# Two linear-attention and gMLP layers on one core: ScalarE issues the stores of the turned rows and of the gelu rows

## The chip, the core and the metric

The kernel runs on one core of one Trainium2 chip. The metric is the device time of one execution in microseconds. The core has a matrix engine (TensorE, PE in the profile), three engines for element-wise work (VectorE, DVE; ScalarE, ACT; GpSimd, POOL), and a sync engine (SyncE, SP) that computes nothing and here issues most of the DMAs. Every engine runs its own list of instructions in order. What ties the lists together are semaphores: an instruction waits until the semaphores of what it needs have reached given values. A DMA is issued by the instruction list of one engine (an instruction of its own, which first waits for what it has to read), runs beside the engines, and raises a semaphore when it has landed.

## The reference

Two pairs of layers, each with a layer norm ahead and a residual around it, on `x` of 2048 tokens by 512 features, all in fp32. First linear attention with 32 heads of 16 features:

```python
pq, pk = phi(q), phi(k)                       # phi(t) = (t + 1 if t > 0 else exp(t)) + 1e-6
kv  = einsum("bhsd,bhse->bhde", pk, v);  z = sum of pk over s
num = einsum("bhqd,bhde->bhqe", pq, kv); den = einsum("bhqd,bhd->bhq", pq, z) + 1e-6
x = x + (num / den) @ wo
```

Then a gMLP block with 2 x 896 inner features:

```python
z = gelu(layernorm(x) @ w_in);  z1 = z[..., :896];  z2 = layernorm(z[..., 896:])
g = einsum("ts,bsf->btf", w_sp, z2) + b_sp[None, :, None]
x = x + (z1 * g) @ w_out
```

Both blocks run twice with the same weights.

## The kernel before

**Precision.** Every fp32 product is made of three matmuls: both operands are split into a high and a low half, and `mm3` (L150 to L152) adds high·high, high·low and low·high. A high half is a copy on ACT (`high`, L136), a low half a subtraction on DVE (`low`, L139). So nearly every operand of PE passes through ACT and then DVE.

**Stages of a layer.** P1 goes over the 16 token tiles of 128 rows for K, Q and the sums of the attention. P2 goes over them again (`P2.run`, the token steps, step `s` from 1 to 18): it finishes attention, and makes the two halves of the gMLP's expansion. P4 multiplies by `w_sp` and then `w_out`. In the profile the token steps of layer 0 lie at about 155 to 330 us, those of layer 1 at about 838 to 1012 us.

**A token step** works on several token tiles at different stages. In program order, for a step `s` in the middle:

- `b(s)`: take the turned rows of attention's numerator for tile `s`, split them (ACT L136, DVE L139 on pages `pg`); `c(s-1)`: multiply the tile before by the folded weights (12 matmuls, 128x512); `c2`: DVE adds the result to the residual (L849); `c_stats`: the norm's statistics (DVE L265, L267, POOL L269 to L274).
- `a2(s+2)`: divide by the denominator (DVE L806 to L817) and store the rows for turning (`qt`, on SP).
- `c3(s-1)`: store the new residual (L857, on SP), normalise on ACT into a tile `z_turn` (L280), and store that for turning (`yt`, L316).
- `d(s-2)`: take the turned rows of an earlier `yt`, split them into `qd` (ACT L136, DVE L139); `e(s-3)`: multiply `qd` by the second half of the expansion's weights (24 matmuls, the form 128x448); `e2` to `e4`: gelu (ACT L906), sum of squares (L915), norm of an earlier tile (L280 on `z_z`).
- `f`, up to twice: one feature tile of the first half of the expansion, computed transposed for four token tiles at once (12 matmuls), gelu on ACT (L941), and a store to DRAM (L944), which P4 loads later. The target is a tile `z_out` for the first one in a step and a page `pg` for the second.
- `make.step` (layer 0 alone): sums of weight pieces, split on ACT and DVE and stored by SP (L231); loads for the steps to come.

**Turning.** A tile must be transposed between the two products. `Turn` does this for most tiles by way of DRAM: `store` (L316) writes the 128x512 rows as four blocks, `load` reads them back in another order, and DVE transposes blocks of 32x32 (L331). There are three kinds: `xt` in P1, `qt` and `yt` in P2. For `yt` (`xturn`) the tiles 0 to 3 of each layer are turned by PE instead, so 12 tiles per layer are stored and loaded.

**Order.** The program is written out by hand in this order; nothing reorders it. Each engine takes its instructions from the common text. Pages (`pg`, 23 of them) and other buffers are reused, and an instruction that writes one waits for the last reader, also when that is a DMA. Each DMA raises one of eight semaphores ("lanes", DMAHW0 to DMAHW7 for those of SP and ACT), and it waits for the DMA that used its lane before.

In the tail of the steps and in P4's start, `gelu_out` (L949 to L953) makes the same kind of gelu row; there the store is already issued by ACT (L952).

Of the kernel before, what the change touches and what calls it, by code (L numbers as in the profile page):

```python
# [91 lines left out]
def mixer_kernel(ctx: ExitStack, tc: tile.TileContext, x_in, wqkv, wo_d, win1_d, win2_d, wsp_d, bsp_d, wout_d,  # L92
                 ident_d, mask_d, out_d):
    nc = tc.nc
# [15 lines left out]
    def ztag(i, shape, kind, dtype=F32):  # L110
        t = main.tile(shape, dtype, tag=f"z{i}", bufs=1, name=f"z{i}_{kind}")
        ztile[i] = t
        return t
# [14 lines left out]
    z1s = {}  # L128
# [19 lines left out]
    def mm3(out, a, b, start, stop):  # L148
        (ah, al), (bh, bl) = a, b
        nc.tensor.matmul(out, ah, bh, start=start, stop=False)  # L150
        nc.tensor.matmul(out, ah, bl, start=False, stop=False)  # L151
        nc.tensor.matmul(out, al, bh, start=False, stop=stop)  # L152

    class Weight:


        def __init__(self, slots, shape, pieces, turned=False):
            self.slots, self.shape, self.pieces, self.turned = slots, shape, pieces, turned
            self.h = self.l = None
            self.raw = deque()  # L160
            self.n_load = self.n_split = 0
# [42 lines left out]
    class Make:  # L204
# [22 lines left out]
        def store(self, g):  # L227
            m = 2 * len(self.raw[g])
            h, l, p = self.part.pop(g)
            for n, t in enumerate((h, l)):  # L230
                nc.sync.dma_start(kept[:, m:m + 2, g, n, :], t.rearrange("p (m f) -> p m f", m=2))  # L231
            pages.put(p, l, lag=STORE)
# [21 lines left out]
    def w_in1():  # L254
        return Weight(bigs, [P, NF, 4, P], [win1_d[f] for f in range(NF)])
# [29 lines left out]
    def feats(ap, turned):  # L285

        return ap.rearrange("p (g c j) -> p c g j" if turned else "p (c g j) -> p c g j", g=4, c=4)
# [7 lines left out]
    class Turn:  # L295

        def __init__(self, name, by_pe, always=False):
            self.name, self.by_pe, self.always = name, by_pe, always  # L300
            self.held, self.d, self.raw = {}, {}, {}

        def turned(self, i):
# [3 lines left out]
        def store(self, i, src):  # L307
            if i in self.by_pe:
                if self.always:
                    s = pages.get(PAGE)  # L310
                    nc.scalar.activation(feats(s, False), feats(src, True), AF.Copy)
                    src = s
                self.held[i] = src
                return
            d = self.d[i] = dram.tile([512, P], F32, name=f"{self.name}_{i}")
            nc.sync.dma_start(d.rearrange("(g n) f -> n g f", g=4), src.rearrange("p (g f) -> p g f", g=4))  # L316

        def load(self, i):
            if i in self.d:
                self.raw[i] = load(self.d.pop(i).rearrange("(p m) f -> p (m f)", m=4))  # L320
# [452 lines left out]
    class P2:  # L773
        def __init__(self, p1):
            self.L = L = p1.L
            self.p1 = p1
            self.win1, self.win2 = w_in1(), p1.win2
            self.qturn, self.xturn = Turn(f"qt{L}", range(3), True), Turn(f"yt{L}", range(4))
            self.qp, self.qT, self.x, self.ms, self.xB, self.z, self.zms = {}, {}, {}, {}, {}, {}, {}
            self.fq = deque()  # L780
            self.fnext = []
            self.held = deque()
            self.S, self.T, self.Tp, self.X, self.zmean = {}, {}, {}, {}, {}
# [145 lines left out]
        def f(self, tag=None):  # L929
            if not self.fq:  # L930
                return False
            n, f = self.fq.popleft()
            h, l = self.xT[n]
            w = self.win1
            b = banks.get(PAGE)
            for c in range(4):
                mm3(b, (w.h[:, f, c, :], w.l[:, f, c, :]), (h[:, c, :], l[:, c, :]), c == 0, c == 3)
            if f == NF - 1 and n < 2:
                quads.put(*self.xT.pop(n))
            t = pages.get(PAGE) if tag is None or tag >= NT else ztag(tag, PAGE, "out")  # L940
            nc.scalar.activation(t, b, AF.Gelu_apprx_tanh)  # L941
            banks.put(b)
            z1s[self.L, n, f] = dram.tile(PAGE, F32, name=f"z1_{self.L}_{n}_{f}")
            nc.sync.dma_start(z1s[self.L, n, f], t)  # L944
            if id(t) in pages.held:
                pages.put(t, lag=STORE)
            return True
# [983 lines left out]
```

## Time and profile before

| | |
|---|---|
| median of 3 runs | 1363.74 us (1363.53 to 1364.71) |
| profiled execution | 1365.79 us, of which the span of the profile is 1364.1 us |
| PE busy | 1355.8 us (99%) |
| DVE, ACT, POOL busy | 991.1 us (73%), 676.3 us (50%), 484.0 us (35%) |
| granted TensorE clock, mean | 0.998 |
| DMA | 310.18 MB, mean 227 GB/s |
| `yt` stores | 24 of 256 KB, issued by SP, 2.6 us to landing (median) |
| gelu stores of L944 | 32 of 256 KB, issued by SP, 2.0 and 2.1 us to landing (medians) |
| gelu stores of L952 | 24 of 256 KB, issued by ACT, 3.2 us to landing (median) |

How to read the rows. A row of the timeline has the start in us from the span's start, the duration in us, engine, line, instruction, output and inputs by name, shapes, and in brackets the engine's idle time just before, with what ended it. `SPq` and `ACTq` are the instruction lists themselves, which issue DMAs. A row of the waits reads: who waited, for whom, us in total, times, longest. A row of the chain has start, duration and what; for a DMA the duration runs from its issue to its landing. A row of the windows has the stretch, its length, the busy time of PE, PE's weight loads, DVE, ACT and POOL with the number of instructions, the granted clock of TensorE, the busy share of the DMA engines and GB/s.

### The profile page before, as it was taken

How to read it: one execution, taken by the hardware profiler on the slowest of the kernel's cores; microseconds unless marked ns; L12 is line 12 of the kernel's file. 1: busy time of each engine (PE TensorE's matmuls, PEld its weight loads, DVE VectorE, ACT ScalarE, POOL GpSimd, SP SyncE). 2: the span in 40 equal slices, each digit the busy share in tenths (PEclk: the TensorE clock that was granted, in tenths of full speed). 3: DMA queues.
4: the chain of work that ended last, by engine and by line, in shares of the span. 5: the costliest groups of instructions: out<-in, count | busy, mean ns of one | idle time of the engine just before them, and what ended most of it. 6: DMA issues, size and time to landing. Idle time of an engine off the chain costs nothing.

```text
span 1364.1 us, 18420 instructions
## 1 busy us (share of the span) xinstructions
PE 1355.8 (99%) x6087; PEld 1133.3 (83%) x6087; DVE 991.1 (73%) x1518; ACT 676.3 (50%) x1149; POOL 484.0 (35%) x594
## 2 busy tenths in 40 slices
PE   9999999999999999999999999999999999999998
PEld 7888888878888888888888888888888888888887
DVE  7985777666866797976678757776757798978642
ACT  6875555456543343442456655555665534533310
POOL 2333376543276247426421133533220011412240
PEclk9999999999999999999999999999999999999999
DMA  5862478876698888795776534666577698569552
GB/s 186 243 204 88 124 258 290 275 254 188 210 345 297 285 287 281 269 370 185 229 255 196 192 96 124 190 225 226 202 215 269 195 324 323 195 198 314 218 183 87
DMA packets 181744, 310.18 MB, mean 227 GB/s; under 512 B 15696, under 2 KB 67920, under 8 KB 177552
## 3 DMA queue, kind: packets, MB, share of 16 engines
q1 hardware_dynamic: 166544, 251.45, 56.2%
q0 software_dynamic: 11504, 51.12, 10.4%
q10 hardware_dynamic: 3600, 6.42, 1.3%
q8 instruction: 48, 0.79, 0.2%
q14 instruction: 48, 0.39, 0.1%
HBM read 211.68 MB, written 97.26 MB: 226 GB/s over the span
## 4 chain that ended last, share of the span: by engine, by line
PE 88%; DVE 4%; ACT 3%; DMA 2%; issue 1%; POOL 1%; DVEq 0%; ACTq 0%; POOLq 0%; SPq 0%
PE bank L152 15%; PE bank L150 15%; PE bank L151 15%; PE bank L1631 9%; PE bank L1632 9%; PE bank L1633 9%; PE bank L1562 4%; PE bank L1564 4%; PE bank L1565 4%; PE bank L1008 1%; PE bank L1009 1%; PE bank L1007 1%; DVE pg L331 1%; DMA pg<-yt 1%; DMA yt<-z_turn 1%
## 5 line engine op out<-in xcount | busy, mean ns | idle before, releaser
L1631 PE MATMUL bank<-qd,pg 128*128 128x512 f32 x544 | 211.6, 389 | 0.0
L1632 PE MATMUL bank<-qd,pg 128*128 128x512 f32 x544 | 211.6, 389 | 0.0
L1633 PE MATMUL bank<-qd,pg 128*128 128x512 f32 x544 | 211.6, 389 | 0.0
L1478 DVE TENSOR_TENSOR qd<-qd,qd 128x1024 fp32r<-128x1024 f32 x104 | 141.7, 1363 | 64.4 <-ACT qd L1469 64.1
L1469 ACT ACTIVATE qd<-qd 128x1024 fp32r<-128x1024 f32 x104 | 110.1, 1059 | 133.3 <-DVE qd L1478 41.0
L152 PE MATMUL bank<-qd,pg 128*128 128x512 f32 x380 | 148.8, 391 | 0.1
L136 ACT ACTIVATE pg<-pg 128x512 fp32r<-128x512 f32 (+1 forms) x146 | 89.7, 620 | 109.8 <-DVE pg L331 36.8
L139 DVE TENSOR_TENSOR pg<-pg,pg 128x512 fp32r<-128x512 f32 (+1 forms) x143 | 107.7, 753 | 29.7 <-ACT pg L136 24.8
L1653 POOL TENSOR_TENSOR bg<-bg,pg 128x512 f32<-128x512 f32 x56 | 89.4, 1607 | 108.6 <-DMA pg<-z 100.0
L1633 PEld LDWEIGHTS bank<-qd,pg 128*128 128x128 f32 x544 | 102.1, 188 | 21.3
L1631 PEld LDWEIGHTS bank<-qd,pg 128*128 128x128 f32 x544 | 102.1, 188 | 21.1
L1632 PEld LDWEIGHTS bank<-qd,pg 128*128 128x128 f32 x544 | 102.1, 188 | 21.1
L1221 POOL TENSOR_TENSOR pg<-pg,pg 128x512 f32<-128x512 f32 x50 | 77.3, 1545 | 107.9 <-DMA pg<-in_wsp_dram 92.1
L150 PE MATMUL bank<-qd,pg 128*128 128x512 f32 x284 | 110.8, 390 | 0.0
L151 PE MATMUL bank<-qd,pg 128*128 128x512 f32 x284 | 110.6, 389 | 0.0
L150 PE MATMUL bank<-bg,qd 128*128 128x448 f32 x256 | 94.9, 371 | 1.9 <-ACT qd L136 1.9
L331 DVE STREAM_TRANSPOSE pg<-pg 128x512 f32<-128x512 f32 x79 | 86.3, 1093 | 13.6 <-DMA pg<-yt 11.6
L152 PE MATMUL bank<-bg,qd 128*128 128x448 f32 x256 | 94.5, 369 | 0.4 <-DVE qd L139 0.2
L151 PE MATMUL bank<-bg,qd 128*128 128x448 f32 x256 | 94.2, 368 | 0.0
L269 POOL TENSOR_SCALAR rs<-mv 128x1 f32<-128x1 f32 x63 | 31.7, 504 | 168.3 <-DVE mv L267 165.0
L150 PE MATMUL bank<-wo,qd 128*128 128x512 f32 x224 | 87.1, 389 | 0.0
L1562 PE MATMUL bank<-qd,pg 128*128 128x512 f32 x224 | 87.1, 389 | 0.0
(227 smaller groups left out, 3234.5 us busy)
## 6 DMA issues: line engine op xcount, KB each, us to landing
qd<-s SPq DMA_DIRECT2D x64, 512.0 KB, 4.1
qd<-n POOLq DMA_DIRECT2D x32, 1024.0 KB, 8.0
pg<-in_wsp_dram SPq DMA_DIRECT2D x92, 256.0 KB, 4.9
qd<-in_wsp_dram SPq DMA_DIRECT2D x40, 512.0 KB, 4.6
pg<-z SPq DMA_DIRECT2D x56, 256.0 KB, 4.1
n<-pg SPq DMA_DIRECT2D x55, 256.0 KB, 4.3
x<-pg SPq DMA_DIRECT2D x48, 256.0 KB, 2.7
pg<-x SPq DMA_DIRECT2D x48, 256.0 KB, 3.5
```

What stands on the lines that cost most here:

```text
L136: nc.scalar.activation(h, src, AF.Copy)
L139: nc.vector.tensor_sub(l, src, h.bitcast(F32))
L150: nc.tensor.matmul(out, ah, bh, start=start, stop=False)
L151: nc.tensor.matmul(out, ah, bl, start=False, stop=False)
L152: nc.tensor.matmul(out, al, bh, start=False, stop=stop)
L331: nc.vector.transpose(y.rearrange("p c (t m) -> p m c t", m=4), r.rearrange("p (m c j) -> p m c j", m=4, c=4))
L1469: nc.scalar.activation(wh, r, AF.Copy)
L1478: nc.vector.tensor_sub(wl, r, wh.bitcast(F32))
L1562: m(out[i], h[:, o, f], w[:, o, 0], start=first and name in ("P1", "P2", "P5"), stop=False, skip_group_check=True)
L1631: m(out, h[:, o], w[:, 0, j, :], start=start, stop=False, skip_group_check=True)
L1632: m(out, h[:, o], w[:, 1, j, :], start=False, stop=False, skip_group_check=True)
L1633: m(out, l[:, o], w[:, 0, j, :], start=False, stop=stop, skip_group_check=True)
```

## The change

`Turn` gets an argument for the engine that issues its stores; P2 passes ScalarE for `yt`, while `xt` and `qt` stay on SP. The store of `f` is issued by ScalarE too. The loads stay on SP.

```diff
-        def __init__(self, name, by_pe, always=False):
-            self.name, self.by_pe, self.always = name, by_pe, always
+        def __init__(self, name, by_pe, always=False, issue=nc.sync):
+            self.name, self.by_pe, self.always, self.issue = name, by_pe, always, issue
...
-            nc.sync.dma_start(d.rearrange("(g n) f -> n g f", g=4), src.rearrange("p (g f) -> p g f", g=4))
+            self.issue.dma_start(d.rearrange("(g n) f -> n g f", g=4), src.rearrange("p (g f) -> p g f", g=4))
...
-            self.qturn, self.xturn = Turn(f"qt{L}", range(3), True), Turn(f"yt{L}", range(4))
+            self.qturn, self.xturn = Turn(f"qt{L}", range(3), True), Turn(f"yt{L}", range(4), issue=nc.scalar)
...
-            nc.sync.dma_start(z1s[self.L, n, f], t)
+            nc.scalar.dma_start(z1s[self.L, n, f], t)
```

PE, DVE and POOL keep their instructions and their order. ACT's list grows by 56 stores, SP's shrinks by the same 56. Below is ACT's list in layer 0's step 12 (the step that begins at 268.97 us), before, from the normalisation into `z_turn` to the split of the next tile; in square brackets the semaphores that an instruction waits for:

```order
L280 ACTIVATE z10_turn_3025<-pg18_302_2686,nb_3016,rs_3013 128x4x4x32 [waits Pool_49]
L280 ACTIVATE z8_z0_2917<-z8_z0_2917,znb_2942,zrs_2941 128x896 [waits Activation_49]
L906 ACTIVATE z9_z0_3062,acc_3063<-bank6_99_3036 128x448 [waits DMAHW2_49,PE_49]
L906 ACTIVATE z9_z0_3062,acc_3063<-bank7_100_3049 128x448 [waits PE_49]
L941 ACTIVATE z14_out_3081<-bank4_101_3068 128x512 [waits PE_49]
L915 ACTIVATE pg16_335_3088,ss_3085<-z9_z0_3062,nm_3066 128x896 [waits DMAHW6_49,DVE_49]
L941 ACTIVATE pg12_336_3106<-bank0_102_3093 128x512 [waits DMAHW7_49,PE_49]
L136 ACTIVATE pg8_337_3112<-pg1_299_2680 128x512 [waits DMAHW3_49]
L136 ACTIVATE pg16_344_3132<-pg13_343_3130 128x512 [waits DVE_49,Activation_49]
```

The same place in the changed kernel:

```order
L280 ACTIVATE z10_turn_3025<-pg18_302_2686,nb_3016,rs_3013 128x4x4x32 [waits Pool_49]
L316 DMA yt0_11_3027<-z10_turn_3025 128x4x128 [waits DMAHW3_49,Activation_49]
L280 ACTIVATE z8_z0_2917<-z8_z0_2917,znb_2942,zrs_2941 128x896
L906 ACTIVATE z9_z0_3062,acc_3063<-bank6_99_3036 128x448 [waits PE_49]
L906 ACTIVATE z9_z0_3062,acc_3063<-bank7_100_3049 128x448 [waits PE_49]
L941 ACTIVATE z14_out_3081<-bank4_101_3068 128x512 [waits PE_49]
L944 DMA z1_0_1_4_3083<-z14_out_3081 128x512 [waits DMAHW7_49,Activation_49]
L915 ACTIVATE pg16_335_3088,ss_3085<-z9_z0_3062,nm_3066 128x896 [waits DMAHW4_49,DVE_49]
L941 ACTIVATE pg12_336_3106<-bank0_102_3093 128x512 [waits PE_49]
L944 DMA z1_0_1_5_3108<-pg12_336_3106 128x512 [waits DMAHW3_49,Activation_49]
L136 ACTIVATE pg8_337_3112<-pg1_299_2680 128x512
L136 ACTIVATE pg16_344_3132<-pg13_343_3130 128x512 [waits DVE_49,Activation_49]
```

Three stores now stand between the activations, each with two waits: for the activation just ahead of it, and for the DMA that used its lane before. The lane of the second z store (DMAHW3) is that of the `yt` store four activations earlier.

SP's list at the same place before, from the store of the `qt` rows to the load of the turned `yt` rows:

```order
L316 DMA qt0_14_3019<-pg21_321_2883 128x4x128 [waits DMAHW0_49,DVE_49]
L857 DMA x1_11_87<-pg18_302_2686 128x512 [waits DMAHW1_49]
L316 DMA yt0_11_3027<-z10_turn_3025 128x4x128 [waits DMAHW2_49,Activation_49]
L944 DMA z1_0_1_4_3083<-z14_out_3081 128x512 [waits DMAHW3_49,Activation_49]
L944 DMA z1_0_1_5_3108<-pg12_336_3106 128x512 [waits DMAHW4_49,Activation_49]
L231 DMA win1_sums_124<-pg7_324_2967 128x2x256 [waits DMAHW5_49]
L231 DMA win1_sums_124<-pg19_300_2682 128x2x256 [waits DMAHW6_49]
L132 DMA pg15_338_3115<-yt0_11_3027 128x512 [waits DMAHW7_49,DMAHW2_49,PE_49]
```

And in the changed kernel:

```order
L316 DMA qt0_14_3019<-pg21_321_2883 128x4x128 [waits DMAHW0_49,DVE_49]
L857 DMA x1_11_87<-pg18_302_2686 128x512 [waits DMAHW1_49]
L231 DMA win1_sums_124<-pg7_324_2967 128x2x256 [waits DMAHW2_49,Activation_49]
L231 DMA win1_sums_124<-pg19_300_2682 128x2x256 [waits DMAHW4_49]
L132 DMA pg15_338_3115<-yt0_11_3027 128x512 [waits DMAHW5_49,DMAHW3_49,PE_49]
```

The three stores are gone from SP's list, and the load of the turned rows (L132) follows two stores of `make` directly. The loads that come after it keep their order.

## Prediction

> **What bounds the kernel.** I read the page first, then who waits for whom on TensorE, then ACT and DVE in order of time in the token steps, and last SP.
>
> ```profile
> PE 1355.8 (99%) x6087; PEld 1133.3 (83%) x6087; DVE 991.1 (73%) x1518; ACT 676.3 (50%) x1149; POOL 484.0 (35%) x594
> PE   9999999999999999999999999999999999999998
> ```
>
> TensorE (PE) is busy for 1355.8 of 1364.1 us. So there is next to nothing to win, and every microsecond for which PE is made to wait is lost. What it waits for today:
>
> ```profile
> PE bank L150 <- ACT qd L136: 1.9, 2, 1.6
> PE bank L152 <- DVE qd L139: 0.2, 1, 0.2
> ```
>
> Both are operands of the matmul `e`, and they come out of the token steps. These two rows hold the only waits that this change can touch. Whether the new work on ACT is free depends on how much earlier than needed those operands are ready. DVE's L139 writes the low half of `qd`; L152 on a 128x448 form is the first matmul that reads it.
>
> ```profile
> 216.49 0.99 DVE L139 TENSOR_TENSOR qd<-pg,qd 128x512 fp32r<-128x512 f32 x1 [0.70 <-ACT qd L136]
> 230.63 1.21 DVE L139 TENSOR_TENSOR qd<-pg,qd 128x512 fp32r<-128x512 f32 x1 [0.70 <-ACT qd L136]
> 221.35 0.36 PE L152 MATMUL bank<-bg,qd 128*128 128x448 f32 x1
> 231.89 0.47 PE L152 MATMUL bank<-bg,qd 128*128 128x448 f32 x1
> 258.48 0.47 PE L152 MATMUL bank<-bg,qd 128*128 128x448 f32 x1 [0.23 <-DVE qd L139]
> 282.07 0.47 PE L150 MATMUL bank<-bg,qd 128*128 128x448 f32 x1 [0.37 <-ACT qd L136]
> 293.18 0.47 PE L150 MATMUL bank<-bg,qd 128*128 128x448 f32 x1 [1.57 <-ACT qd L136]
> ```
>
> In layer 0 the operand of the matmul at 221.35 was ready at 216.49 + 0.99 = 217.48, a lead of 3.87 us. For the next one it was ready at 231.84 and read at 231.89: the lead is gone. From there on PE runs on the heels of ACT and DVE, with 0.23, 0.37 and at last 1.57 us of waiting. So in the second half of layer 0's steps, whatever delays ACT and DVE delays PE.
>
> What ACT and DVE do in one such step (ACT first, then DVE):
>
> ```profile
> 268.97 0.63 ACT L136 ACTIVATE qd<-pg 128x512 fp32r<-128x512 f32 x1 [4.10 <-DVE pg L331]
> 269.51 0.80 ACT L280 ACTIVATE z_turn<-pg,nb,rs 128x512 f32<-128x512 f32 x1
> 270.22 1.12 ACT L280 ACTIVATE z_z<-z_z,znb,zrs 128x896 f32<-128x896 f32 x1
> ...
> 272.28 0.59 ACT L941 ACTIVATE z_out<-bank 128x512 f32<-128x512 f32 x1
> 272.76 1.04 ACT L915 ACTIVATE pg<-z_z,nm 128x896 bf16<-128x896 f32 x1
> ...
> 273.78 0.59 ACT L941 ACTIVATE pg<-bank 128x512 f32<-128x512 f32 x1
> 274.26 0.63 ACT L136 ACTIVATE pg<-pg 128x512 fp32r<-128x512 f32 x1
> ...
> 281.38 0.63 ACT L136 ACTIVATE qd<-pg 128x512 fp32r<-128x512 f32 x1 [4.04 <-DVE pg L331]
> ```
>
> ```profile
> 274.93 0.69 DVE L139 TENSOR_TENSOR pg<-pg,pg 128x512 fp32r<-128x512 f32 x1 [2.30 <-ACT pg L136]
> 275.54 1.08 DVE L331 STREAM_TRANSPOSE pg<-pg 128x512 f32<-128x512 f32 x1
> ...
> 280.27 1.08 DVE L331 STREAM_TRANSPOSE pg<-pg 128x512 f32<-128x512 f32 x1
> ```
>
> This is a ring. ACT works without a pause from z_turn (L280) to the high half of `make` (L136, 274.26 to 274.89). DVE waits 2.30 us for that, works without a pause from 274.93 to the transpose L331 at 280.27, and ACT waits 4.04 us for the transpose. One turn is 12.41 us (268.97 to 281.38), with no spare time in it. PE's two full steps from 231.89 to 258.48 took 26.6 us, 13.3 each and hardly any of it waiting, so the ring gains less than 1 us a turn on PE at best. ACT's share of 50% on the page says nothing about that: its idle time is the time in which it waits for the other half of the ring.
>
> **The change, part by part.** SP loses 56 stores (24 of turned rows, 32 of gelu rows), ACT gains them; no computation moves. I price one store on ACT by the only place that has such a pattern today, the gelu of layer 0's tail, whose store ACT already issues:
>
> ```profile
> 306.47 0.62 ACT L950 ACTIVATE pg<-pg 128x512 f32<-128x512 f32 x1
> 307.12 0.35 ACTq L952 DMA_DIRECT2D z<-pg  x1
> 307.51 0.60 ACT L1015 ACTIVATE pg<-bank 128x512 f32<-128x512 f32 x1 [0.42 <-ACT pg L950]
> 283.35 0.37 SPq L316 DMA_DIRECT2D yt<-z_turn  x1
> ```
>
> From the start of the gelu to the start of the next activation pass 1.04 us. Between two gelu-type activations with no store between them it is 0.48 (272.28 to 272.76) to 0.52. The store waits for the end of its activation, takes 0.33 to 0.35 us to issue, and the overlap of two activations is lost: 0.52 to 0.56 us. A yt store is 0.37 us to issue on SP, so 0.80 + 0.03 + 0.37 + 0.04 for z_turn and store, against 0.71 (269.51 to 270.22): 0.53. I take 0.53 for each. The bounds for one store: nothing, where ACT would wait there anyway, and 1 us, twice the row, where it also meets a busy queue.
>
> *Layer 0.* All three stores of a full step (yt after z_turn, two z after the two L941) lie in the stretch of ACT that DVE waits for. Up to the wait at 293.18 these are the stores of yt 4 to 12 and of 14 z pages: 23 x 0.53 = 12.2 us on the ring. Some of it falls into waits that exist:
>
> ```profile
> 196.84 0.63 ACT L136 ACTIVATE pg<-pg 128x512 fp32r<-128x512 f32 x1 [0.49 <-DVE pg L331]
> 206.95 1.04 ACT L915 ACTIVATE pg<-z_z,nm 128x896 bf16<-128x896 f32 x1 [0.26 <-DVE nm L909]
> 281.92 0.80 ACT L280 ACTIVATE z_turn<-pg,nb,rs 128x512 f32<-128x512 f32 x1
> 291.39 1.08 DVE L331 STREAM_TRANSPOSE pg<-pg 128x512 f32<-128x512 f32 x1 [2.30 <-DMA pg<-yt]
> ```
>
> ACT waits 0.49 and 0.26 us there; I double that for what DVE may give in the same steps: 1.5 us of cover, an estimate. The 2.30 us of DVE are a wait for a yt load, whose data this store brought:
>
> ```profile
> 283.35 5.30 DMA yt<-z_turn
> ```
>
> z_turn had ended at 282.72 and SP issued the store 0.63 us later; landing took 5.30 us. If it again takes 5.30, 2.30 - 0.63 = 1.7 us are cover for ACT's stores; if it lands faster, all of it. So the ring brings the operand of 293.18 later by 12.2 - 1.5 - 2.3 = 8.4 to 12.2 - 1.5 - 1.7 = 9.0 us. There PE has no lead, so all of it reaches PE. Already at 231.89, behind ten of these stores, it is some 4 us. I take 8.5 for layer 0, with ends at 6 (0.43 us a store) and 11 (no cover but 1.5).
>
> The Trainium skill (DMA: Bandwidth & Descriptors, "Issuing engines are not separate DMA queues") says that DMAs of different engines run on the same 16 DMA engines, and that spreading them saves only the sequencer's time to start them. By that rule the 5.30 us stay and layer 0 costs 9.0; a queue of ACT's own that passes the others would make it 8.4. No row of before shows which.
>
> *Layer 1* has no `make`, and its ring is shorter, so the lead is larger:
>
> ```profile
> 881.64 1.37 DVE L139 TENSOR_TENSOR pg<-pg,pg 128x512 fp32r<-128x512 f32 x1 [0.65 <-ACT pg L136]
> 906.88 0.69 DVE L139 TENSOR_TENSOR pg<-pg,pg 128x512 fp32r<-128x512 f32 x1 [0.56 <-DMA z<-pg]
> 904.79 0.32 SPq L944 DMA_DIRECT2D z<-pg  x1
> 910.88 1.12 DVE L331 STREAM_TRANSPOSE pg<-pg 128x512 f32<-128x512 f32 x1 [1.17 <-DMA pg<-yt]
> 912.70 0.69 DVE L139 TENSOR_TENSOR qd<-pg,qd 128x512 fp32r<-128x512 f32 x1 [0.70 <-ACT qd L136]
> 915.22 0.36 PE L152 MATMUL bank<-bg,qd 128*128 128x448 f32 x1
> ```
>
> At 881.64 DVE waits 0.65 us for ACT, so ACT's stores are on the ring here too. At 906.88 DVE waits 0.56 us for the landing of the z store issued at 904.79, because it writes into that page: a store that goes out later holds DVE up. Five yt and six z stores lie ahead of the operand that DVE ends at 912.70 + 0.69 = 913.39: 5.8 us, of which I let 0.9 fall into waits. PE reads it at 915.22, a lead of 1.82 us. That leaves 3.1 us of waiting, and PE pays for a wait twice:
>
> ```profile
> 294.80:298.20 3.40, 3.40 (x10) 2.98 (x10) 1.24 (x2) 3.05 (x9) 0.64 (x2) 0.50 0.47 128
> ```
>
> Behind the wait of 1.57 us the granted clock is 0.50 for 3.4 us, half of which, 1.7 us, is lost. So layer 1 is 4.8 us by this sum. Against it stands that DVE waits 1.17 us at 910.88 for a yt load, which SP issues behind the z stores; without them it goes out earlier, and where such waits set the pace the stores are covered. I take 4.0, with ends at 0 and 8. In layer 0 half clock changes nothing, since PE then waits for the ring anyhow, and before paid it too.
>
> The Trainium skill (TensorE: Matmul & The Clock Gate, "Why this matters for your kernels") warns of gaps over about 3 us. By that figure a wait of 1.57 us should not have brought the half clock; the row shows that it did, and the measurement decides. By the page's figure layer 1 would be about 2 us cheaper.
>
> *SP* is relieved of the waits for ACT in front of its loads, and of 56 issues of 0.32 to 0.37 us. That is worth only what the yt loads are worth, which is counted above: no load makes PE wait elsewhere. The steps outside of the two stretches keep their code and order.
>
> **Sum.** The profiled execution took 1365.79 us (span 1364.1). 1365.79 + 8.5 + 4.0 = 1378.3; it lies 2.05 us above the median of 1363.74, so the changed kernel's median comes to 1376.2 us.
>
> **Rivals.**
> *Layer 1 hides its stores*, by loads that come earlier: 1363.74 + 8.5 = 1372.2. For it: the 1.17 us at 910.88. Against: 881.64. It is part of the main case's range.
>
> *Faster, by SP's relief.* The yt store goes out at once and the yt load is not queued behind z stores, so the wait at 293.18 goes: 1.57, with 0.37 and 0.23 before it and 1.7 of half clock, 3.9 us in all: 1359.9. For it: the 5.30 us of that store, and SP's late issue. It holds only if a store costs the ring less than about 2.3 / 23 = 0.1 us; the tail's row says 0.53. The Trainium skill's section on issuing engines calls that issue time usually small beside the DMA, which is the reading behind this rival; here 0.53 us is small beside 5.30 us of transfer, and large beside a lead of 0.05.
>
> *Same.* ACT idles 4 us in each turn, the stores move into that: 1363.7. Against: the stores stand ahead of what DVE waits for, not in the idle part.
>
> *Dearer, since ACT waits for landings.* The built program lets each store also wait for an earlier DMA of its semaphore lane, up to now on SP. The second z store of a step often has the yt store of its own step there:
>
> ```profile
> 274.40 0.32 SPq L944 DMA_DIRECT2D z<-pg  x1
> 276.38 0.33 SPq L132 DMA_DIRECT2D pg<-yt  x1
> ```
>
> The load at 276.38 went out when that yt store landed, 1.95 us after the z store's issue; with 1.06 us of stores ahead of it ACT would wait 0.9 us. At five to eight such places of 1 to 1.5 us it adds some 8 us: 1384.
>
> **How the numbers follow.** Both layers as summed, or layer 1 partly hidden: 0.72. Landing waits on top: 0.15. Same: 0.05. Faster: 0.08. The likeliest gives 1376.2; its own range is 1370 to 1381. The range of 1366 to 1385 takes in a store at a fifth of its price at the lower end and the landing waits at the upper, and leaves out the same and faster cases. A change of under 0.2% (2.7 us) can't be told from none. Slower 0.87, same 0.05, faster 0.08.
>
> **What would show it.** PE's waits for `qd` L136 and L139 between 225 and 300 grow from 2 us to over 6, and new ones stand near 915. An ACT step shows yt and z stores with 1.0 to 1.25 us from activation to next activation; DVE's wait for L136 grows from 2.30 to nearly 3.9, and a turn from 12.4 to 14. It is wrong if the turn stays at 12.4, if a store costs ACT under 0.2 us, or if PE's waits shrink. Landing waits would show as ACT idle behind a store's semaphore for a DMA.

## The result, and the profile after

The changed kernel takes 1387.54 us (median of 4 runs, 1385.66 to 1389.35); the kernel before took 1363.95 us beside it (1363.53 to 1364.71). The ratio is 1.0172, with a 95% interval of 1.0155 to 1.0190: slower by 23.6 us. Forecast were 12.5 us. The profiled execution took 1387.61 us, its span is 1385.9 us, 21.8 us above the span before.

TensorE's waits (what it waited for: us in total, times, longest), and its busy time on the page:

```profile
PE bank L150 <- ACT qd L136: 7.4, 4, 2.6
PE bank L150 <- ACT pg L136: 3.0, 2, 2.3
PE bank L152 <- DVE qd L139: 2.8, 5, 0.6
PE bank L152 <- DVE pg L139: 1.7, 3, 0.8
```

```profile
PE 1364.4 (98%) x6087; PEld 1135.5 (82%) x6087; DVE 984.6 (71%) x1518; ACT 680.4 (49%) x1149; POOL 479.0 (35%) x594
```

The waits for L136 and L139 have grown from 2.1 to 14.9 us, and PE's busy time by 8.6 us, with the same 6087 matmuls. A part of that is half clock: the granted clock falls to 0.50 for 3.4 us at four places (from 238.4, 296.5, 931.3 and 985.9 us) instead of at one, an estimated 1.7 us lost at each, so some 5 us. Where the rest comes from was not looked into.

Both layers pay, and about the same. PE's list of matmuls is in the same order in both traces, so the start of one matmul can be compared. The 2500th, past layer 0's token steps, starts 10.7 us later than before, the 4000th, ahead of the critical stretch of layer 1, 10.7 us, and the last 21.8 us. So layer 0 costs 10.7 us and layer 1 costs 11.1 us; the sum of the prediction had 8.5 and 4.0.

**Layer 0** does in the main what was forecast. One step of ACT, and DVE's wait for its end:

```profile
279.61 0.63 ACT L136 ACTIVATE qd<-pg 128x512 fp32r<-128x512 f32 x1 [4.12 <-DVE pg L331]
280.14 0.80 ACT L280 ACTIVATE z_turn<-pg,nb,rs 128x512 f32<-128x512 f32 x1
280.98 0.38 ACTq L316 DMA_DIRECT2D yt<-z_turn  x1
281.40 1.14 ACT L280 ACTIVATE z_z<-z_z,znb,zrs 128x896 f32<-128x896 f32 x1 [0.46 <-ACT z_turn L280]
...
283.48 0.60 ACT L941 ACTIVATE z_out<-bank 128x512 f32<-128x512 f32 x1
284.10 0.33 ACTq L944 DMA_DIRECT2D z<-z_out  x1
284.53 1.04 ACT L915 ACTIVATE pg<-z_z,nm 128x896 bf16<-128x896 f32 x1 [0.46 <-ACT z_out L941]
...
285.57 0.58 ACT L941 ACTIVATE pg<-bank 128x512 f32<-128x512 f32 x1
286.18 0.33 ACTq L944 DMA_DIRECT2D z<-pg  x1
286.55 0.63 ACT L136 ACTIVATE pg<-pg 128x512 fp32r<-128x512 f32 x1 [0.40 <-ACT pg L941]
...
293.67 0.63 ACT L136 ACTIVATE qd<-pg 128x512 fp32r<-128x512 f32 x1 [4.10 <-DVE pg L331]
```

```profile
287.22 0.69 DVE L139 TENSOR_TENSOR pg<-pg,pg 128x512 fp32r<-128x512 f32 x1 [3.39 <-ACT pg L136]
```

The three stores stand in the row, each with 0.33 to 0.38 us of issue. From `z_turn` to `z_z` it is now 1.26 us (0.71 before), from the first gelu to the square 1.05 (0.48), from the second gelu to the copy 0.98 (0.48): 0.55, 0.57 and 0.50 a store, where 0.53 was priced. DVE waits 3.39 us instead of 2.30, and a turn of the ring takes 14.06 us (279.61 to 293.67) instead of 12.41.

**Layer 1** does something else. What DVE waits for among the DMAs, before and then after, over the whole program:

```profile
DVE pg L331 <- DMA pg<-yt: 11.6, 9, 2.3
DVE pg L139 <- DMA z<-pg: 2.6, 3, 1.5
```

```profile
DVE pg L331 <- DMA pg<-yt: 2.3, 2, 1.4
DVE pg L139 <- DMA z<-pg: 12.8, 5, 3.8
```

SP's relief is real: DVE's waits for turned rows fall from 11.6 to 2.3 us. But a second row has grown from 2.6 to 12.8 us. It is DVE's low half of a split, which writes into the page out of which the second gelu store of the step is still being read. Before, that was 0.56, 0.60 and 1.47 us at three places of layer 1, the first at 906.88. Now there is one in layer 0 (the first row), and the three of layer 1 are the same instructions as before:

```profile
216.64 0.69 DVE L139 TENSOR_TENSOR pg<-pg,pg 128x512 fp32r<-128x512 f32 x1 [2.31 <-DMA z<-pg]
924.09 0.69 DVE L139 TENSOR_TENSOR pg<-pg,pg 128x512 fp32r<-128x512 f32 x1 [3.17 <-DMA z<-pg]
963.53 0.69 DVE L139 TENSOR_TENSOR pg<-pg,pg 128x512 fp32r<-128x512 f32 x1 [3.84 <-DMA z<-pg]
978.27 0.69 DVE L139 TENSOR_TENSOR pg<-pg,pg 128x512 fp32r<-128x512 f32 x1 [3.28 <-DMA z<-pg]
```

Why the store lands so late is seen in SP's and ACT's issues around the second of these:

```profile
918.23 0.32 SPq L132 DMA_DIRECT2D pg<-yt  x1
918.65 0.41 SPq L132 DMA_DIRECT2D pg<-x  x1
919.49 0.32 SPq L132 DMA_DIRECT2D pg<-qt  x1
```

```profile
919.98 0.33 ACTq L944 DMA_DIRECT2D z<-pg  x1
```

Before, SP had to wait for the second gelu, issued its store (904.79, in the prediction) and only then its loads:

```profile
906.68 0.49 SPq L132 DMA_DIRECT2D pg<-yt  x1
907.27 0.42 SPq L132 DMA_DIRECT2D pg<-x  x1
```

So the store went out ahead of these loads, and DVE could go on at 906.88. Now SP does not wait for the gelu any more. Its three loads of 256 KB go out at 918.23 to 919.49, ahead of the store at 919.98, and the store lands 4.0 us after its issue, as the chain of the changed kernel has it:

```profile
919.98 4.03 DMA z<-pg
```

The views of the line L944, before and after, give the landings of all 32 gelu stores:

```profile
DMA to landing us min/median/max: 2.0/2.0/4.3
```

```profile
L944 ACTq EVENT_SEMAPHORE  x31: 17/17/17, 192.2 to 1030.2; - x31
DMA to landing us min/median/max: 2.1/3.9/8.1
```

The median from issue to landing goes from 2.0 to 3.9 us. The first line after is for the rival of the prediction in which ACT itself waits for landings, through a semaphore: at 31 stores ACT's semaphore instruction takes 17 ns, the shortest and the longest. So no gelu store waits on ACT for a landing.

Behind these waits PE waits in layer 1, where it waited nowhere before, 5.9 us in all; the two long ones:

```profile
930.00 0.47 PE L150 MATMUL bank<-bg,qd 128*128 128x448 f32 x1 [2.59 <-ACT qd L136]
984.16 0.47 PE L150 MATMUL bank<-bg,qd 128*128 128x448 f32 x1 [2.48 <-ACT qd L136]
```

### The profile page after: what moved, and what is told of

It is laid out like the page before. It is cut to its first block, busy times and chain, and to the rows that moved or that the text cites. A ratio compares the mean times of both kernels' runs of the same rounds, so it can differ in the third digit from the quotient of the medians.

```text
span 1385.9 us, 18404 instructions
## 1 busy us (share of the span) xinstructions
PE 1364.4 (98%) x6087; PEld 1135.5 (82%) x6087; DVE 984.6 (71%) x1518; ACT 680.4 (49%) x1149; POOL 479.0 (35%) x594
## 4 chain that ended last, share of the span: by engine, by line
PE 78%; ACT 7%; DVE 6%; issue 3%; POOL 3%; DMA 2%; ACTq 1%; SPq 0%; DVEq 0%; POOLq 0%
PE bank L152 12%; PE bank L150 11%; PE bank L151 11%; PE bank L1631 9%; PE bank L1632 9%; PE bank L1633 9%; PE bank L1562 4%; PE bank L1564 4%; PE bank L1565 4%; DMA z<-pg 2%; DVE pg L331 1%; ACT z_z L906 1%; PE bank L1008 1%; PE bank L1009 1%; PE bank L1007 1%
## 5 line engine op out<-in xcount | busy, mean ns | idle before, releaser
L136 ACT ACTIVATE pg<-pg 128x512 fp32r<-128x512 f32 (+1 forms) x146 | 89.4, 619 | 113.1 <-DVE pg L331 30.5
L139 DVE TENSOR_TENSOR pg<-pg,pg 128x512 fp32r<-128x512 f32 (+1 forms) x143 | 105.8, 740 | 49.2 <-ACT pg L136 32.5
L1633 PEld LDWEIGHTS bank<-qd,pg 128*128 128x128 f32 x544 | 102.1, 188 | 21.4
L1631 PEld LDWEIGHTS bank<-qd,pg 128*128 128x128 f32 x544 | 102.1, 188 | 21.1
L1632 PEld LDWEIGHTS bank<-qd,pg 128*128 128x128 f32 x544 | 102.1, 188 | 21.1
L150 PE MATMUL bank<-bg,qd 128*128 128x448 f32 x256 | 97.4, 381 | 7.6 <-ACT qd L136 7.4
L152 PE MATMUL bank<-bg,qd 128*128 128x448 f32 x256 | 96.9, 379 | 2.9 <-DVE qd L139 2.8
L151 PE MATMUL bank<-bg,qd 128*128 128x448 f32 x256 | 96.0, 375 | 0.0
L331 DVE STREAM_TRANSPOSE pg<-pg 128x512 f32<-128x512 f32 x79 | 86.1, 1090 | 3.7 <-DMA pg<-yt 2.3
L152 PEld LDWEIGHTS bank<-qd,pg 128*128 128x128 f32 x380 | 71.3, 188 | 20.7 <-DVE pg L139 6.1
```

Of the source, the lines that this page charges most:

```text
L136: nc.scalar.activation(h, src, AF.Copy)
L139: nc.vector.tensor_sub(l, src, h.bitcast(F32))
L331: nc.vector.transpose(y.rearrange("p c (t m) -> p m c t", m=4), r.rearrange("p (m c j) -> p m c j", m=4, c=4))
L1631: m(out, h[:, o], w[:, 0, j, :], start=start, stop=False, skip_group_check=True)
L1632: m(out, h[:, o], w[:, 1, j, :], start=False, stop=False, skip_group_check=True)
L1633: m(out, l[:, o], w[:, 0, j, :], start=False, stop=stop, skip_group_check=True)
```

## The experiments

Two theories stood against each other. The *ring theory* is the prediction's: the issue time of the stores on ACT, 0.53 us each, is all that costs. The *landing theory* adds that SP's loads now run ahead of the gelu stores, that these land later, and that DVE waits for their landing because it writes into their pages.

The results, with the lateness of PE's 2500th matmul (layer 0) and of the last one against the 4000th (layer 1), each against the same matmuls of the profile before. These two columns are from one profiled execution each. A profile of the unchanged layer 0 came out 1.6 to 1.9 us earlier twice (layer 1 only; pages in the kernel before), because PE's long wait there was shorter (1.07 us in one of them) and no half clock followed. So differences of 2 us in the column of layer 0 are not to be read. The unchanged layer 1 came out at 0.0 three times.

| kernel | median, us | ratio to before (95%) | layer 0 | layer 1 |
|---|---|---|---|---|
| the change | 1387.54 | 1.0172 (1.0155 to 1.0190) | 10.7 | 11.1 |
| layer 0 only | 1375.28 | 1.0081 (1.0066 to 1.0096) | 9.3 | 0.0 |
| layer 1 only | 1374.92 | 1.0078 (1.0063 to 1.0093) | -1.9 | 10.8 |
| turned rows only | 1369.14 | 1.0037 (1.0022 to 1.0051) | 2.5 | 1.0 |
| gelu rows only | 1377.38 | 1.0097 (1.0082 to 1.0112) | 5.7 | 5.9 |
| 2 KB on ACT, stores on SP | 1375.87 | 1.0071 (1.0051 to 1.0091) | 6.7 | 3.9 |
| the change, SP held by 2 KB | 1381.49 | 1.0114 (1.0093 to 1.0135) | 9.9 | 6.2 |
| the change, pages kept 12 | 1376.34 | 1.0077 (1.0061 to 1.0094) | 8.6 | 2.5 |
| before, pages kept 12 | 1364.54 | 0.9997 (0.9988 to 1.0007) | -1.6 | 0.0 |
| first gelu stores only | 1368.02 | 1.0022 (1.0010 to 1.0034) | 4.0 | 0.2 |
| second gelu stores only | 1370.38 | 1.0042 (1.0027 to 1.0057) | 1.1 | 2.5 |
| all stores on POOL | 1394.12 | 1.0215 (1.0191 to 1.0239) | 20.7 | 6.3 |
| earlier load of turned rows | 1368.08 | 1.0021 (1.0012 to 1.0031) | 2.5 | 0.0 |

**The layers apart.** The change in one layer, the stores of the other stay on SP.

```diff
-            nc.sync.dma_start(z1s[self.L, n, f], t)
+            (nc.scalar if self.L == 0 else nc.sync).dma_start(z1s[self.L, n, f], t)
```

(and the same for `issue` of `xturn`; the second kernel with `self.L == 1`)

> The change in layer 0 alone (23 stores ahead of the last wait, and the stores of the tail of its steps). In the trace of the changed kernel PE runs about 11 us late from 300 us on, up to 912 us, where layer 1's waits begin. If the two layers are independent, this kernel takes 1364 + 11 = 1375 us. Ring theory (the issue time of the stores on ACT is all that costs): 1372.5, the 8.5 us of the prediction. Landing theory (DVE also waits for the landing of the second gelu store of a step, into whose page it writes): 1375, with one such wait of about 2.7 us at 216 us.

> The change in layer 1 alone. Ring theory: 4 to 5 us, 1368. Landing theory: three DVE waits of 3 to 4 us for the landing of z stores (2.6 us in the kernel before, 12.8 us in the changed one) stand in layer 1's steps, and PE waits twice for 2.5 us and runs at half clock behind each: 11 to 12 us, 1375.

Measured: 10.9 and 10.6 us above the kernel before. Both sizes are those of the landing theory, and their sum, 21.5 us, is near the 23.6 us of the whole change. So the layers are independent or nearly so, and layer 1 is more than twice what the prediction gave it.

This profile of layer 1 alone also says what the half clock is worth. PE's two long waits are there, at the same matmuls as in the whole change, but the clock stays at full speed behind both, and layer 1 still costs 10.8 us (11.1 with the half clock in the whole change). In the window rows the clock is the third number from the end:

```profile
917.43 0.47 PE L150 MATMUL bank<-bg,qd 128*128 128x448 f32 x1 [2.56 <-ACT qd L136]
972.06 0.47 PE L150 MATMUL bank<-bg,qd 128*128 128x448 f32 x1 [2.58 <-ACT qd L136]
917.40:937.40 20.00, 19.92 (x92) 17.13 (x93) 14.78 (x27) 11.61 (x23) 4.65 (x10) 1.00 0.70 224
972.00:992.00 20.00, 19.88 (x90) 16.78 (x91) 12.88 (x21) 12.10 (x25) 4.13 (x12) 1.00 0.52 172
```

Where the half clock is missing, PE has one more wait, of 1.40 us at 966.91. So layer 1's cost does not hang on the half clock.

**The kinds of stores apart.** One of the two lines of the change alone.

```diff
+            self.qturn, self.xturn = Turn(f"qt{L}", range(3), True), Turn(f"yt{L}", range(4), issue=nc.scalar)
```

```diff
+            nc.scalar.dma_start(z1s[self.L, n, f], t)
```

> Only the stores of the turned rows on ACT, the gelu stores stay on SP. Ring theory: nine stores of 0.53 us in layer 0 less 1.5 to 3.3 us of cover, and nothing in layer 1, whose lead of 1.8 us takes five stores less 0.9: about 2 to 3 us, 1366.5. Landing theory: the same, since the gelu stores still land at once (1.7 us): 1366.5, with DVE's waits for z landings still at 2.6 us.

> Only the gelu stores on ACT, the turned rows' stay on SP. Ring theory: 14 x 0.53 = 7.4 less 1.5 in layer 0, and 3.2 less 1.8 to 2.7 and a half clock of 1.7 in layer 1: about 8 us, 1372. Landing theory: layer 0 about 8, layer 1 nearly all of its 11.5, since the gelu store's landing is what DVE waits for: 1382, with DVE's waits for z landings near 12 us.

Measured: 1369.14 and 1377.38. The turned rows cost 4.8 us, twice what both theories gave. The profiled executions differ by 3.9 us, of which layer 0 has 2.5 and layer 1 has 1.0. The gelu rows cost 13.0 us, between the two theories' values: more than the ring theory's 8 and less than the landing theory's 18. In layer 1 they cost 5.9 us, though four waits for their landing stand there and in layer 0, as long as in the whole change:

```profile
DVE pg L139 <- DMA z<-pg: 14.5, 4, 4.4
```

The two kinds together cost 5.8 us more than their sum of 17.8 us. Most of the difference lies in layer 1: 5.9 + 1.0 against 11.1, where layer 0 has 5.7 + 2.5 against 10.7. It looks as if a lead that covers one of them cannot cover both.

The same kernels give the price of a store on the ring of layer 0, by the start of `qd`'s high half in two following steps: 272.47 and 285.45 us with the turned rows only, 263.25 and 276.70 us with the gelu rows only. A turn takes 12.41 us without stores, 12.98 with one and 13.45 with two, and 14.06 with three: 0.57, 0.52 and 0.55 a store.

**Only the issue on ACT.** The kernel before, and behind each of the 56 stores a second DMA of 2 KB on ACT (and likewise behind the `yt` store):

```diff
             nc.sync.dma_start(z1s[self.L, n, f], t)
+            nc.scalar.dma_start(dram.tile([1, 512], F32, name=f"dz_{self.L}_{n}_{f}"), t[0:1, :])
```

> The kernel before, with all stores on SP, and behind each of the 56 activations a second DMA of 2 KB (one row of the stored tile, into memory that nothing reads) issued by ACT. ACT pays the issue, SP and the stores stay as they were. Ring theory (the issue time on ACT is all): the whole loss, 1387. Landing theory: layer 0 about 8.5 to 9 us, layer 1 the 3 to 5 us by which 5.8 us of issues exceed its lead, with the half clock: 1376 to 1378, with a gelu store landing in 1.7 us and DVE's waits for z landings near 3 us.

Measured: 1375.87, 10.5 us above the kernel before beside it, as the landing theory has it. A small DMA is a little cheaper for ACT than a store: 0.23 us of issue, and 0.43 us of a turn (13.70 against 12.41 us with three of them). One of the three:

```profile
279.98 0.59 ACT L943 ACTIVATE z_out<-bank 128x512 f32<-128x512 f32 x1
280.60 0.23 ACTq L947 DMA_DIRECT2D dz<-z_out  x1
280.93 1.04 ACT L917 ACTIVATE pg<-z_z,nm 128x896 bf16<-128x896 f32 x1 [0.36 <-ACT z_out L943]
```

From gelu to square it is 0.95 us against 0.48. Scaled by 0.53 / 0.43, as an estimate, its 6.7 us in layer 0 would be 8.3 us and its 3.9 us in layer 1 would be 4.8 us: close to the prediction's sum of 8.5 and 4.8 ahead of its last discount. This is the ring's part alone, and it is about half of what the change costs (10.5 of 23.6 us as measured).

**Only the order of the loads.** The changed kernel, and SP gets back something to wait for: a DMA of 2 KB at the place of each store it lost. It computes and stores the same.

```diff
             nc.scalar.dma_start(z1s[self.L, n, f], t)
+            nc.sync.dma_start(dram.tile([1, 512], F32, name=f"dz_{self.L}_{n}_{f}"), t[0:1, :])
```

> The changed kernel, with a DMA of 2 KB from the same tile issued by SP at the place where SP issued the store before. So SP waits for ACT as before and its loads stay behind the store's place. If the stores land late because SP's loads now share the DMA engines with them, the second gelu store lands in about 2 us again instead of 3.8 to 5.1, DVE's waits for z landings fall from 12.8 to under 6 us, and the time to 1378 to 1381. If ACT's queue itself lands later, nothing changes: 1387.

Measured: 1381.49, 16.1 us above the kernel before beside it, where the change is 23.6 us above, although SP has 56 DMAs more. That is half a microsecond above the 1378 to 1381 expected, and well under the 1387 of a slow queue of ACT. Here are ACT's second gelu store of a step, then SP's small DMA and its load of turned rows, DVE's row, and DVE's waits in all (a line L333 here is L331 of the changed kernel):

```profile
919.62 0.33 ACTq L946 DMA_DIRECT2D z<-pg  x1
```

```profile
919.62 0.22 SPq L947 DMA_DIRECT2D dz<-pg  x1
921.43 0.59 SPq L132 DMA_DIRECT2D pg<-yt  x1
```

```profile
921.76 0.69 DVE L139 TENSOR_TENSOR pg<-pg,pg 128x512 fp32r<-128x512 f32 x1 [1.18 <-DMA z<-pg]
```

```profile
DVE pg L139 <- DMA z<-pg: 3.6, 3, 1.2
DVE pg L333 <- DMA pg<-yt: 11.9, 8, 2.3
```

The store that ACT issues at 919.62 has landed by 921.76, when DVE goes on, in 2.1 us instead of 4.0 (this trace gives no landings of its own). The waits for gelu landings are back at 3.6 us. So ACT's queue is not slow; the store was late because SP's loads had gone out ahead of it. The kernel with the first gelu stores only (below) agrees. There too ACT issues the first store of a step, SP still waits for the second gelu, and the 16 stores that ACT issues land in

```profile
DMA to landing us min/median/max: 2.0/2.0/5.0
```

In exchange the waits for turned rows are back at 11.9 us, which is what SP's relief had taken away.

**Only the wait for the landing.** The changed kernel, with a stored gelu page kept out of use for 12 allocations instead of 6. Instructions and their order are the same, only which page a tile gets differs.

```diff
-                pages.put(t, lag=STORE)
+                pages.put(t, lag=12)
```

> The changed kernel, with a stored gelu page kept out of use for 12 allocations of pages instead of 6, so that DVE's low half of a split no longer writes into a page whose store is in flight. ACT issues exactly what it issues in the changed kernel. Ring theory: 1387, as the changed kernel. Landing theory: the three waits of 3.2 to 3.8 us in layer 1 and the 2.7 us in layer 0 go: layer 1 falls from 11 to 3 to 5 us, layer 0 by about 2, 1378 to 1380.

> The control for the run with 12 allocations: the kernel before, all stores on SP, and only the gelu pages kept out for 12 allocations. DVE's three short waits for z landings (2.6 us in all) go, but no PE wait stands behind them in the kernel before. Landing theory: 1364, within 0.2%. If the other pages by themselves make the program faster, and not the landings, it is 5 to 10 us under that.

Measured: 1376.34 against 1365.37, and the same edit in the kernel before changes nothing (0.9997, 0.9988 to 1.0007). So other pages bring nothing by themselves, and in the changed kernel they bring 12.6 us (23.6 less 11.0, each against its own runs of the kernel before; 10.7 us by the two profiled executions). Given the intervals of both ratios, it is about half of the change's cost and not more exact than that. DVE's split no longer meets a store in flight:

```profile
919.40 0.69 DVE L139 TENSOR_TENSOR pg<-pg,pg 128x512 fp32r<-128x512 f32 x1 [0.54 <-ACT pg L136]
```

This row has the place of 924.09 in the changed kernel. It waits for ACT's high half, and the next turned rows are there when it needs them. Layer 0 costs 8.6 us in this profile and layer 1 costs 2.5 us. What the change costs without the landing waits is 11.0 us; the sum of the prediction, which had none, was 12.5.

**First against second stores of a step.** The same number of stores, 16, on ACT. The first ones of a step come out of `z_out`, the second ones out of pages.

```diff
+            (nc.sync if id(t) in pages.held else nc.scalar).dma_start(z1s[self.L, n, f], t)
```

(and the two engines exchanged)

> Of the gelu stores only the first of each step (out of its own z_out buffer, which nothing needs soon) on ACT; the second and the turned rows stay on SP. Ring theory: eight stores of 0.53 us less 1.5 us of cover in layer 0, next to nothing in layer 1: 2 to 3 us, 1367. Landing theory: the same, 1367, since SP still waits for the second gelu before its loads, and the second store lands in 1.7 us.

> Of the gelu stores only the second of each step (out of a page that DVE soon writes into) on ACT, as many stores as in the run with the first ones, or fewer. Ring theory: 2 us, 1366.5. Landing theory: SP's loads go out ahead of it, it lands in 3.5 to 5 us, DVE waits 3 to 4 us at three places of layer 1 and at one of layer 0: about 2 + 2 + 5 us, 1373, and at least 4 us above the run with the first stores.

Measured: 1368.02 and 1370.38. The first is near what both theories gave. The second lies between the ring theory's 1366.5 and the landing theory's 1373: the second stores cost more, but 2.4 us more and not the 4 expected. The waits are there, and they are long:

```profile
DVE pg L139 <- DMA z<-pg: 9.7, 3, 4.1
```

9.7 us of DVE's waiting in layer 1, and it costs 2.5 us. With few stores on ACT the ring of layer 1 has enough in hand for most of it. So a landing wait as such is not the price either, but what remains of it after the lead; in the whole change the other stores have used up the lead. The profile with layer 0 only has the same: in its unchanged layer 1 DVE waits 2.94 us for a gelu landing at 965.20, and PE loses nothing (0.0).

**All stores on POOL**, which takes the issue off both SP and ACT (`nc.gpsimd` in the place of `nc.scalar` in both lines of the change):

```diff
-            nc.scalar.dma_start(z1s[self.L, n, f], t)
+            nc.gpsimd.dma_start(z1s[self.L, n, f], t)
```

> All 56 stores issued by POOL instead of ACT. Neither SP nor ACT carries them. If SP's relief is worth something once ACT does not pay, the waits of DVE for loads of turned rows go and the time is under 1364, at best 1360. Landing theory: SP's loads run ahead here too, the stores land later than 1.7 us, and layer 1 pays part of its landing waits: 1366 to 1372. POOL also has to wait for ACT in front of each store, and the row statistics that DVE and ACT need stand behind on POOL; if that decides, it is over 1380.

Measured: 1394.12, the slowest, and in the third of the cases expected. ACT issues none of these stores, and yet it is worse, above all in layer 0 (20.7 us):

```profile
DVE pg L139 <- DMA z<-pg: 17.5, 5, 4.5
```

A first gelu store takes POOL 0.55 to 0.60 us, and the waits for gelu landings are the longest of all (17.5 us in 5 waits). Whether POOL's own time or these waits decide was not separated. SP's relief is not a gain here either.

**The load of turned rows earlier**, the one version that the profiles suggested as better than the kernel before, since SP issues this load late:

```diff
+                self.xturn.load(s - 1)
                 self.f(SPARE_TAGS.get(s) if self.L == 0 else None)
...
-                self.xturn.load(s - 1)
```

> No store is moved to ACT; in SP's order the load of the turned row stands ahead of the second gelu store instead of behind it and behind the split's DMAs. If the turned row's load is what holds layer 0's ring at the one long wait of the kernel before (2.30 us of DVE, 1.57 us of PE and 1.7 us of half clock behind it), 1361 to 1363. Landing theory: the load then shares the DMA engines with the gelu stores, and where SP waits for the turned row's landing the second gelu store goes out later; if that decides, 1366 to 1370.

Measured: 1368.08, slower by 0.21% (0.12 to 0.31%), inside the 1366 to 1370 of the landing theory. The long wait at the end of layer 0 did not go, it grew, from 1.57 to 3.54 us (at 295.71).

Why it grew stays open. None of the versions beats the kernel before.

## Why the prediction was wrong, point by point

- *PE pays for whatever delays ACT and DVE in the second half of layer 0's steps.* Right. All of layer 0's 10.7 us came in between 216 and 300 us of the kernel before.
- *A store costs ACT 0.53 us on the ring.* Right: 0.52 to 0.57 in turns with one, two and three stores. Turn 14.06 us (14 forecast), DVE's wait 3.39 us (3.9 forecast).
- *Layer 0: 12.2 less 1.5 and 1.7 to 2.3 of cover, 8.5.* Right for the ring: 8.6 us with the landing wait gone, and 4.3 us at the matmul of 231.89, for which some 4 us were forecast. That the end agrees to 0.1 us is partly luck, since a half clock more or less moves this column by 1.7 us. The 2.30 us of DVE's wait for turned rows was covered as forecast. Measured were 10.7, and at 231.89 it was 6.6 us: the one landing wait at 216.64 (2.31 us) came on top, which the sum did not have. This split of layer 0 rests on one profile each.
- *Layer 1: 5.8 less 0.9 and a lead of 1.82, with a half clock, taken as 4.0, at most 8.* Wrong: 11.1. This is the term that failed. Its ring part was right in size (2.5 us with the landing waits gone, 3.9 with small DMAs on ACT). What it left out stood in its own text: "a store that goes out later holds DVE up", at 906.88. The sum has no term for it, and so priced it at nothing, without a reason: as if a gelu store went on landing about 2 us after its issue. But that time hung on SP's order. SP's wait for the gelu kept its loads behind the store; without that wait they went ahead, the landing took 4.0 us, and three waits of 0.6 to 1.5 us became 3.2 to 3.8 us. They grew by 7.7 us in all, and PE waited 5.9 us in layer 1, where it had not waited before. With the pages kept out of use for longer DVE's landing waits went, and layer 1 fell from 11.1 to 2.5 us.
- *SP's relief is worth only what the turned rows' loads are worth.* Wrong as a whole, right as to that gain. The gain came (11.6 to 2.3 us), but the stores landed later behind the loads that went out earlier, and that cost more than the gain.
- *The rival of landing waits, 1384, at 0.15.* Close in size and wrong in its place: it had ACT waiting at its semaphores, which never happened. DVE waited, through a page used again. That rival came from looking at what the moved store waits for; who waits for the moved store was the question that decided.
- *The rivals of the same time and of a gain by SP's relief.* False. The relief without the landing waits still leaves the kernel at 1376.34, and without any cost on ACT, on POOL, at 1394.12.
- *PE pays for a wait twice, by the half clock (1.7 us in layer 1's sum).* Not a rule. In the profile of the whole change it came behind both long waits of layer 1. In that of layer 1 alone it came behind neither, and layer 1 cost 10.8 us all the same. So it is not what made layer 1 dear.

What stays open: which of POOL's costs decides, why the earlier load made layer 0's long wait longer, and why the gelu rows alone cost layer 1 only 5.9 us with landing waits as long as in the whole change; that the lead was spent only once is argued from the sizes and was not tried by itself.

## What to carry to other kernels

When a DMA moves to another engine's list, two things move: its issue time goes to the new engine, and the old engine loses a wait, so that what stands behind it there is issued earlier and can delay the landing of others. Look for who waits for the moved DMA's landing, above all through a buffer that is soon used again, and price that wait with the new neighbours and not with the old landing time. Costs beside a lead do not add up: two halves of the change that cost layer 1 about 1 and 6 us alone cost it 11 us together. If a store must move anyway, keep its buffer out of use for longer; that was worth about half of the 23.6 us here, and made no difference in the kernel before, where such waits were short.

## What was unexpected of the hardware

- A 256 KB store took 2.0 us from issue to landing (median of 32) where SP issued it ahead of its own loads, and 3.9 us (median, up to 8.1) in the changed kernel, where ACT issued it and SP's loads no longer stayed behind; the one followed above took 4.0 us behind three such loads. On ACT's queue it took 2.0 us (median of 16) as long as SP's loads were held back. The Trainium skill (DMA: Bandwidth & Descriptors, "Issuing engines are not separate DMA queues") says that DMAs of several engines share 16 engines and interleave; these runs agree. It adds that spreading them saves only the sequencer's time; here it also changed the order in which they were issued, and that was about half of the loss.
- The length of a wait alone does not decide on the half clock. Behind the wait of 2.59 us of the changed kernel PE's clock falls to 0.50 for a while, and likewise behind that of 2.48. Behind waits of 2.56 and 2.58 us at the same two matmuls, in the kernel with layer 1 only, it stays at 1.00 (rows above), and so it does behind one of 2.02 us in the kernel with SP held. In the kernel before, 1.57 us had been enough. The row for the changed kernel (window, length, busy times of the engines, granted clock, DMA share, GB/s):

```profile
932.00:934.00 2.00, 2.00 (x7) 1.78 (x6) 1.41 (x3) 1.54 (x4) 0.00 (x0) 0.50 0.16 42
```

The Trainium skill (TensorE: Matmul & The Clock Gate, "Why this matters for your kernels") puts the limit at gaps of about 3 us. The gaps named here are all shorter, and some of them brought the half clock.
